# Three small edits to the order of work in a fused attention and mixer kernel: a transposed row by DMA, one relu on another engine, the last product's third tile whole

## The chip, the cores and the metric

The kernel runs on one core of one Trainium2 chip. A core has TensorE (PE in the profile; its weight loads are PEld), VectorE (DVE), ScalarE (ACT), GpSimd (POOL) and SyncE (SP, which here only issues transfers). PE writes to PSUM, in tiles of 128 partitions and up to 512 f32 to a bank; DVE and ACT read it. The metric is the device time of one execution in microseconds. The kernel before took 740.31 us, the median of three runs (740.12 to 741.42).

## The reference

Attention over 16 query and 4 key heads, then a mixer block over its output. B = 8 batches, S = 384 tokens, head size 64, model width 1024, hidden width 4096.

```python
# attention: x[b, s, h*64 + d]
k = np.repeat(k, 4, axis=1); v = np.repeat(v, 4, axis=1)
scores = np.matmul(q, k.transpose(0, 1, 3, 2)) / np.sqrt(64)
attn = np.exp(scores - np.max(scores, axis=-1, keepdims=True))
attn = attn / (np.sum(attn, axis=-1, keepdims=True) + 1e-09)
x = np.matmul(attn, v)                        # then heads side by side

# mixer
a1 = alpha1 * x + beta1
tok = np.einsum('ts,bsd->btd', w_tok, a1)     # across tokens
u = x + lam * tok
a2 = alpha2 * u + beta2
ch = np.maximum(a2 @ w_ch1, 0.0) @ w_ch2      # across channels
out = u + lam * ch
```

Inputs and output are f32; the kernel multiplies in bf16 and adds up in f32.

## The kernel before

**Tiles.** Tokens lie in NST = 3 tiles of 128, the model width in NP = 8 "rows" p of 128 columns (two heads each), the hidden width in 32 tiles of 128.

**Stages.** Batch 0's attention runs first. Batches 0 and 1 then go through `main(b)`: 32 hidden tiles, each of eight matmuls of 384 columns (L531) into a PSUM tile h with a relu on ACT (L540) or DVE (L542), and then the second layer (L569). The other six batches go in three pairs through `pair(i)`, which takes the two batches' channel layers as 2 x 2 block products with seven products in place of eight (a scheme of Strassen's kind). The first layer's products (L722) go into PSUM tiles X, Y and Z. The second layer's (L786) run in the order `PLACE2`, into tiles called C of 128 x 512, one for each token tile ms: 16 matmuls (t from 0 to 15) of 512 columns for each product and token tile.

**Work woven in.** While the channel layers of two batches run, the attention and the token mix of the next ones are made beside them. `side(b)` gives these pieces with unit numbers, and every `yield` of `main` and `pair` is one unit: at it, the pieces that are due are issued. The pieces of a row p are:

- `scores3`: matmuls (L279) into a tile from `three()` and an exp on ACT (L288). With `later` the third exp of a group is put off into a list.
- `av(p)`: matmuls (L315), then on DVE a reciprocal (L320), the division (L323) and the scaled input of the token mix (L328, L330). At its end the put-off exps are issued (L408, L409).
- `tok_flip(p)`: the token mix, nine matmuls of 128 columns (L340) into a tile from `three()`; DVE reads it (L347: u = x + tok) and scales it to a2 (L351). Then `spill(p)` writes u to the output by a transfer of SP (L243), and a2 is turned, so that channels lie on partitions: by a DMA transpose of SP (L362), or, where `by_pe(p)` says so, later by `turn(p)`.
- `turn(p)`: three transposes on PE (L427) into a tile from `three()`, and a copy on ACT (L429).

In the pairs the next odd batch (5 beside the first pair, 7 beside the second) has turns for its rows 5, 6 and 7, and so has batch 3, which is made beside batch 1's `main`. Nothing is woven into the third pair. Near the end of a pair's work the units are: 74 `turn(5)` and `tok_flip(6)`, 76 `tok_flip(7)`, 77 `turn(6)`, 79 `turn(7)`; the sums of the turned inputs for the next pair (`sums_a`, L586 to L588) follow from unit 76 on.

**PSUM in the second layer of a pair.** Two banks' worth of tiles belong to the pool `acc`; three more pools `sc0`, `sc1`, `sc2` have one tile of two banks each. `three()` hands these out in turn to scores, av, token mix and turns, and leaves sc0 out while `pairs["held"]` is set. Product 4 of the first two pairs is made in two halves (h = 0 with t from 0 to 7, h = 1 with t from 8 to 15), and its three token tiles stay open between them; the third (ms = 2) has sc0, taken at unit 76 in the middle of the tail above. A tile of a pool is given again only when the last reader of the tile before it has finished; the waits for this follow from the order in which tiles are asked for.

**Order.** The order of each engine's instructions is the order in which the code issues them; there is no scheduler that moves them.

**Which engine makes a relu.** A counter `exps[0]` is set by every exp: to 2 behind an exp of batches 1 to 7, to 0 in batch 0. Each hidden tile in `main` lowers it by one and goes to ACT when it is below zero, else to DVE (L538 to L543). So two relus behind an exp go to DVE.

**The last pair's end.** In the last pair every product is made in halves over h, and the products add up in the same PSUM tiles. Product 4 is the last of `PLACE2`. Its third token tile is held as two tiles, columns 0 to 383 (sc1) and 384 to 511 (sc2), so that the first can be finished while the second is multiplied. A finished tile is scaled on DVE (L794), added (L795) and written (L796).

Of the kernel before, what the change touches and what calls it, by code (L numbers as in the profile page):

```python
# [12 lines left out]
def kernel(  # L13
# [36 lines left out]
    NST = S // P  # L50
# [3 lines left out]
    NP = Hq // 2  # L54
    D1 = D + 1
    NPL = 2
# [58 lines left out]
    def by_tok(ap):  # L115
        return ap.rearrange("(p st) d -> p st d", st=NST)
# [91 lines left out]
    late, exps = [], [0]  # L208
# [20 lines left out]
    def side(b):  # L229
# [72 lines left out]
        def av_piece(p, hh):  # L302
            if hh == 0:
                if first:
                    avs[p] = bank([P, 2, NST, D1], "mm", "av")
                else:
                    avs[p] = one().rearrange("p k s -> p (k s)")[:, :2 * NST * D1].rearrange(
                        "p (h st d) -> p h st d", h=2, st=NST)
            av = avs[p]
            hk = (2 * p + hh) // G  # L310
            for sq in range(NST):
                m = NST * hh + sq
                for sk in range(NST):
                    k = (p * NST + sk) * NST + m // 2
                    nc.tensor.matmul(out=av[:, hh, sq, :], lhsT=ess[k // 4][:, m % 2, k % 4, :],  # L315
                                     rhs=vb[:, sk, hk, :], start=(sk == 0), stop=(sk == NST - 1))
            if hh == 0:
                return
            rinv = sb.tile([P, 2, NST, 1], f32, tag="rinv", name="rinv", bufs=1)
            nc.vector.reciprocal(out=rinv, in_=av[:, :, :, D:])  # L320
            if not first:
                xr[p] = sb.tile([P, NST, P], f32, tag="xr", name="xr", bufs=4)
            nc.vector.tensor_tensor(out=x_of(p).rearrange("p st (h d) -> p h st d", h=2), in0=av[:, :, :, :D],  # L323
                                    in1=rinv.to_broadcast([P, 2, NST, D]), op=MUL)
            if first:
                return
            t = sb.tile([P, NST, P], f32, tag="a1f", name="a1f", bufs=1)
            nc.vector.tensor_tensor(out=t, in0=x_of(p), in1=bc(g1, p), op=MUL)  # L328
            a1s[p] = sb.tile([P, NST, P], bf, tag="a1", name="a1", bufs=2)
            nc.vector.tensor_tensor(out=a1s[p], in0=t, in1=bc(h1, p), op=ADD)  # L330
# [74 lines left out]
        def av(p):  # L405
            av_piece(p, 0)
            av_piece(p, 1)
            while late:  # L408
                late.pop(0)()  # L409

        def tok_flip(p):
            tok(p)
            flip(p)
# [5 lines left out]
                a2_transpose(p)  # L419

        def by_pe(p):
            return b % 2 and p >= (NP - 3 if b > NPL else NP - 1)

        def turn(p):
            ps = three()[:, 0].rearrange("p a b -> p (a b)").bitcast(bf)[:, :S].rearrange("p (a b) -> p a b", a=NST)
# [166 lines left out]
    def spare(i):  # L592
        at = 24 * S + i % 3 * 1024
        return hTf[:, at:at + 1024]
# [43 lines left out]
    def free(slot):  # L638
        (w1_free if slot < RING else pad_free).append(slot)
        pump()  # L640
# [29 lines left out]
    def pair(i):  # L670
# [19 lines left out]
        def flush(n=9):  # L690
            while later and n:
                f, *a = later.pop(0)
                f(*a)
                n -= 1

        last = i == NB - 1
# [12 lines left out]
        for g in range(NH // 2):  # L709
            X, Y, snap = {}, {}, {}  # L710
            for k, (o, e) in enumerate(SEQ1):
                t = 2 * g + e
# [47 lines left out]
        def c_banks(ms):  # L760
            return [(0, 512, pairs["sc0"].tile([P, 2, 512], f32, tag="sc", name="C", bufs=1)[:, 0] if ms == NST - 1 else
                     acc.tile([P, 512], f32, tag="acc", name="C", bufs=2))]

        X = [c_banks(ms) if last else None for ms in range(NST)]
        snap = {}
        where = {2: (0, 0), 3: (0, 1), 7: (1, 1), 4: (1, 0)}
        for k, o in enumerate(PLACE2):
            whole = not last and o != 4
            for h in range(1 if whole else 2):
                for ms in range(NST):  # L770
                    if o == 4 and not last and 1 < 3 * h + ms < 5:
                        sum_w1(0, (5, 7, 6)[3 * h + ms - 2])
                    if last and (o, h) in ((6, 1), (7, 0)):
                        (lift_end if o == 7 else begin_end)(ms)
                    if last and (o, h, ms) == (7, 0, NST - 1):
                        X[ms] = [(c0, c1, pairs[sc].tile([P, 2, 512], f32, tag="sc", name="C", bufs=1)[:, 0, :c1 - c0])
                                 for sc, c0, c1 in (("sc1", 0, 384), ("sc2", 384, 512))]
                    if whole:
                        X[ms] = [(0, 512, acc.tile([P, 512], f32, tag="acc", name="C", bufs=2))]
                    elif not last and h == 0:  # L780
                        X[ms] = c_banks(ms)
                        pairs["held"] = ms == NST - 1
                    upto = NH if whole else 8 * h + 8
                    for (c0, c1, x), t in ((c, t) for c in X[ms] for t in range(8 * h, upto)):
                        slot, rhs = w2_slots[i, 4 * k + t // 4], w2_at[i, 4 * k + t // 4]
                        nc.tensor.matmul(out=x, lhsT=hid[:, t, LEFT2[o], ms * P:(ms + 1) * P],  # L786
                                         rhs=rhs[:, t % 4 * 512 + c0:t % 4 * 512 + c1],
                                         start=((not last or o in (1, 6, 7)) and t == 0), stop=(t == NH - 1),
                                         skip_group_check=True)
                        if t % 4 == 3 and ms == NST - 1 and c1 == 512 and not (o == 4 and slot >= RING):  # L790
                            free(slot)
                        if last and o == 4 and t == NH - 1:
                            e, v = ends[ms][:, c0:c1], spare(ms).bitcast(f32)[:, c0:c1]
                            tt(out=v, in0=x, in1=lam_t[:, c0:c1], op=MUL)  # L794
                            tt(out=e, in0=e, in1=v, op=ADD)  # L795
                            nc.sync.dma_start(out=by_tok(out[b0 + 1])[:, ms, c0:c1], in_=e)  # L796
                        if t % 4 == 3 and t < upto - 1 and c1 == 512:
                            q = 4 * ms + t // 4
                            if whole and o in (2, 6) and q in (2, 5, 8, 10):
                                sums_hid(o, (2, 5, 8, 10).index(q))  # L800
                            if t % 8 == 3 and later and (last or later[0][1] != 4):
                                flush(1)
                            yield 1
                    if k == ms == h == 0:
                        pad_free[:] = [RING + 1, RING + 2, RING]
                        pump()
                    if (whole or h == 1) and not (last and o == 4):
                        if o in (1, 6, 5):
                            q = ((1, 6, 5).index(o) * NST + ms) * 512
                            snap[o, ms] = snaps[:, q:q + 512]  # L810
                        else:
                            bb, dw = where[o]
                            t = snap[1, ms] if o == 7 else spare(ms).bitcast(f32)
                        for c0, c1, x in X[ms]:
                            if o == 1:
                                nc.scalar.copy(out=snap[o, ms], in_=x)
                            elif o in (6, 5):
                                tt(out=snap[o, ms], in0=x, in1=snap[1 if last or o == 6 else 6, ms], op=ADD)
                            elif o == 2 and last:
                                tt(out=t, in0=x, in1=lam_t[:, :512], op=MUL)  # L820
                            else:
                                base = {2: 1, 3: 1 if last else 5, 7: 5, 4: 6}[o]
                                tt(out=t[:, c0:c1], in0=x, in1=snap[base, ms][:, c0:c1], op=ADD)
                            if o == 7 and not last:
                                tt(out=snap[6, ms], in0=x, in1=snap[6, ms], op=ADD)
                        if o not in (1, 6, 5):
                            later.append((scaled, o, b0 + bb, ms, dw, t))
                    if last and o in (2, 6) and (h, ms) in ((0, 1), (0, 2), (1, 0), (1, 1)):
                        sums_hid(o, [(0, 1), (0, 2), (1, 0), (1, 1)].index((h, ms)))
                    yield 1  # L830
# [5 lines left out]
    with tc.manual_schedule(engines=order):  # L836
# [162 lines left out]
        for i in range(NB - 1):  # L999
            ps, c = NPL + i, NPL + 2 * i + 2  # L1000
# [56 lines left out]
```

## Time and profile before

| what | value |
| --- | --- |
| runs, median (lowest to highest) | 740.31 us (740.12 to 741.42) |
| the profiled execution | 740.56 us |
| its span, first to last instruction | 738.8 us |
| DMA bytes, mean rate | 151.32 MB, 205 GB/s |
| matmuls of the second layer in pairs (L786), busy | 168.0 and 69.9 us (by where the weights lie) |
| matmuls of the first layer in pairs (L722), busy | 70.2 + 70.2 us into X, 39.0 us into Z |
| exps (L288) on ACT | 126, 1023 ns each |

A profile is one execution taken by the hardware profiler. Its page has the busy time of each engine, the chain of work that ended last, and groups of instructions by line. The trace behind the page also answers for waits (which engine waited for which, how long) and gives a timeline. In the timeline a line begins with the start in microseconds from the span's start and the length; `x8` means eight instructions in a row, and `[0.66 <-DVE hT L542]` that the engine was idle for 0.66 us before it and what ended that. `128x384 bf16<-128x384 f32` are the sizes and types written and read. `SPq` is SP issuing transfers. A matmul's length contains its way through the array, so single ones are longer than the pace at which they follow each other: eight of 512 columns take 1.73 us when they follow back to back, 0.2165 each, and eight of 384 columns 1.30 us.

### The profile page before, as it was taken

How to read it: one execution, taken by the hardware profiler on the slowest of the kernel's cores; microseconds unless marked ns; L12 is line 12 of the kernel's file. 1: busy time of each engine (PE TensorE's matmuls, PEld its weight loads, DVE VectorE, ACT ScalarE, POOL GpSimd, SP SyncE). 2: the span in 40 equal slices, each digit the busy share in tenths (PEclk: the TensorE clock that was granted, in tenths of full speed). 3: DMA queues.
4: the chain of work that ended last, by engine and by line, in shares of the span. 5: the costliest groups of instructions: out<-in, count | busy, mean ns of one | idle time of the engine just before them, and what ended most of it. 6: DMA issues, size and time to landing. Idle time of an engine off the chain costs nothing.

```text
span 738.8 us, 14511 instructions
## 1 busy us (share of the span) xinstructions
PE 731.5 (99%) x5769; PEld 418.8 (57%) x5769; DVE 516.9 (70%) x995; ACT 324.1 (44%) x467; POOL 163.5 (22%) x211
## 2 busy tenths in 40 slices
PE   8999999999999999999999999999999999999997
PEld 5866555566555566655555566655555566654444
DVE  7763366467587889749777988847968988762354
ACT  7632431444333566653334366664343266660000
POOL 9434221420000232211013244020002222000011
PEclk9999999999999999999999999999999999999999
DMA  9999999999899999999989999998989999937965
GB/s 184 194 202 200 207 209 175 185 191 199 204 258 281 177 218 212 268 249 205 297 197 197 202 149 191 204 246 198 274 236 172 211 127 145 172 117 261 293 182 103
DMA packets 218017, 151.32 MB, mean 205 GB/s; under 512 B 88660, under 2 KB 197060, under 8 KB 217948
## 3 DMA queue, kind: packets, MB, share of 16 engines
q0 software_dynamic: 120304, 64.60, 66.6%
q1 hardware_dynamic: 97100, 85.39, 42.9%
q8 instruction: 45, 0.74, 0.4%
q10 hardware_dynamic: 544, 0.39, 0.2%
q14 instruction: 24, 0.20, 0.1%
HBM read 154.84 MB, written 38.27 MB: 261 GB/s over the span
## 4 chain that ended last, share of the span: by engine, by line
PE 95%; DVE 2%; DMA 1%; ACT 0%; issue 0%; DVEq 0%
PE C L786 30%; PE X L722 17%; PE h L531 10%; PE ch L569 10%; PE Y L722 8%; PE sc L279 5%; PE Z L722 4%; PE sc L315 4%; PE sc L340 3%; DMA ops<-a 1%; PE h L223 1%; PE tok L340 1%; PE av L315 0%; PE warm L841 0%; PE tp L265 0%; ACT hT L288 0%
## 5 line engine op out<-in xcount | busy, mean ns | idle before, releaser
L288 ACT ACTIVATE es<-sc 128x1024 bf16<-128x1024 f32 x126 | 121.4, 1023 | 155.9 <-PE sc L279 144.8
L786 PE MATMUL C<-w,arena 128*128 128x512 bf16 (+2 forms) x744 | 168.0, 372 | 0.0
L786 PEld LDWEIGHTS <-arena 128*128 128x128 bf16 x1040 | 94.8, 98 | 100.5 <-issue 5.1
L727 ACT ACTIVATE hT<-X,bias 128x384 f32<-128x384 f32 x144 | 83.7, 581 | 61.6 <-PE X L722 54.9
L722 PEld LDWEIGHTS <-w 128*128 128x128 bf16 x768 | 75.1, 98 | 50.0
L516 POOL DMA_DIRECT2D out_dram<-hT x33 | 28.7, 871 | 284.3 <-DVE hT L687 106.3
L569 PE MATMUL ch<-arena,hT 128*128 128x512 bf16 x384 | 90.8, 379 | 0.0
L185 POOL DMA_DIRECT2D w<-in_moe_w_ch_dram x68 | 62.8, 964 | 98.4 <-PE X L722 34.4
L531 PE MATMUL h<-ops,w 128*128 128x384 bf16 (+1 forms) x480 | 83.3, 327 | 0.8 <-DVE hT L542 0.7
L722 PEld LDWEIGHTS <-pad 128*128 128x128 bf16 x576 | 56.4, 98 | 37.2
L722 PE MATMUL X<-ops,w 128*128 128x384 bf16 x384 | 70.2, 326 | 0.0
L722 PE MATMUL X<-ops,pad 128*128 128x384 bf16 x384 | 70.2, 326 | 0.0
L786 PE MATMUL C<-pad,arena 128*128 128x512 bf16 (+2 forms) x296 | 69.9, 373 | 0.0
L531 PEld LDWEIGHTS <-w 128*128 128x128 bf16 x480 | 45.4, 98 | 30.4 <-issue 2.7
L569 PEld LDWEIGHTS <-hT 128*128 128x128 bf16 x384 | 34.8, 98 | 36.8 <-issue 2.5
L347 DVE TENSOR_TENSOR xr<-sc,xr 128x384 f32<-128x384 f32 x56 | 30.9, 552 | 23.4 <-PE sc L340 23.4
L315 PEld LDWEIGHTS <-es 128*128 128x128 bf16 x1008 | 38.2, 97 | 12.4
L340 PEld LDWEIGHTS <-wtokT 128*128 128x128 bf16 x576 | 37.5, 98 | 11.8 <-DVE a L330 0.8
L279 PE MATMUL sc<-qT,kT 64*128 64x384 bf16 (+2 forms) x576 | 42.0, 272 | 0.8 <-DVE xr L323 0.3
L320 DVE RECIPROCAL rinv<-sc 128x6 f32<-128x6 f32 x56 | 10.7, 192 | 44.3 <-PE sc L315 44.1
L315 PE MATMUL sc<-v,es 128*128 128x65 bf16 x1008 | 39.8, 193 | 0.0
L722 PE MATMUL Z<-ops,w 128*128 128x384 bf16 x192 | 39.0, 326 | 0.0
(138 smaller groups left out, 911.0 us busy)
## 6 DMA issues: line engine op xcount, KB each, us to landing
w<-in_moe_w_ch_dram POOLq DMA_DIRECT2D x68, 512.0 KB, 10.3
w<-w2s SPq DMA_DIRECT2D x60, 512.0 KB, 4.3
pad<-w2s SPq DMA_DIRECT2D x24, 512.0 KB, 8.1
out_dram<-xr SPq DMA_DIRECT2D x56, 192.0 KB, 6.1
out_dram<-hT POOLq DMA_DIRECT2D x33, 256.0 KB, 5.7
arena<-in_moe_w_ch_dram POOLq DMA_DIRECT2D x16, 512.0 KB, 20.0
w2s<-arena SPq DMA_DIRECT2D x28, 256.0 KB, 5.0
q_raw<-in_q_dram POOLq DMA_DIRECT2D x28, 192.0 KB, 10.4
```

What stands on the lines that cost most here:

```text
L185: nc.gpsimd.dma_start(out=w1[:, w1_slots[c]], in_=w1src[:, :, c * CW * P:(c + 1) * CW * P])
L279: nc.tensor.matmul(out=sc[:, hh, k % 4:k % 4 + n], lhsT=kT[r, 2 * p // G, BLK[hh][sk], :], rhs=qT[r, p, st:st + n, :], start=True, stop=True)
L288: nc.scalar.activation(out=e, in_=sc, func=EXP, scale=scale_qk)
L315: nc.tensor.matmul(out=av[:, hh, sq, :], lhsT=ess[k // 4][:, m % 2, k % 4, :], rhs=vb[:, sk, hk, :], start=(sk == 0), stop=(sk == NST - 1))
L340: nc.tensor.matmul(out=ps[:, tt, :], lhsT=wtokT[:, st, tt * P:(tt + 1) * P], rhs=a1s[p][:, st, :], start=(st == 0), stop=(st == NST - 1 an ...
L347: nc.vector.tensor_tensor(out=u, in0=ps, in1=u, op=ADD)
L516: nc.gpsimd.dma_start(out=at, in_=o, accum_op=ADD)
L531: nc.tensor.matmul(out=ps[:, :n], lhsT=w1[:, w1_slots[c], dt, j * P:(j + 1) * P], rhs=a2T[:, dt, :n], start=(dt == 0), stop=(dt == NDT - 1))
L569: nc.tensor.matmul(out=ps, lhsT=hT[:, nt, ms * P:(ms + 1) * P], rhs=w2[:, row(nt)[0], row(nt)[1], cs], start=(i == 0), stop=(i == NNT - 1))
L722: nc.tensor.matmul(out=ps, lhsT=tb[g, o][:, dt, e * P:(e + 1) * P], rhs=opb(LEFT1[o])[:, dt], start=(o in (1, 2, 7) and dt == 0), stop=(dt ...
L727: nc.scalar.activation(out=snap[o, e], in_=ps, func=IDENT, bias=hi if o == 5 else lo)
L786: nc.tensor.matmul(out=x, lhsT=hid[:, t, LEFT2[o], ms * P:(ms + 1) * P], rhs=rhs[:, t % 4 * 512 + c0:t % 4 * 512 + c1], start=((not last o ...
```

## The change

Three edits.

1. Behind a put-off exp the counter is set to 1 and not left at 2, so one relu and not two goes to DVE after it.
2. `by_pe` takes rows 6 and 7, and no longer row 5, in batches 3, 5 and 7. Row 5's a2 is turned by a DMA transpose of SP (L362), issued right behind its spill. `turn(5)`, with its tile from `three()`, is no longer issued.
3. In the last pair's product 4 the third token tile is left out in the first half (h = 0) and gets all its 16 t in the second: columns 0 to 383 for t from 0 to 15, then columns 384 to 511.

```diff
@@ av
             while late:
                 late.pop(0)()
+                exps[0] = 1
@@ by_pe
-            return b % 2 and p >= (NP - 3 if b > NPL else NP - 1)
+            return b % 2 and p >= (NP - 2 if b > NPL else NP - 1)
@@ pair, second layer
             whole = not last and o != 4
+            tail = last and o == 4
             for h in range(1 if whole else 2):
-                for ms in range(NST):
+                for ms in range(NST - (tail and not h)):
...
                     upto = NH if whole else 8 * h + 8
-                    for (c0, c1, x), t in ((c, t) for c in X[ms] for t in range(8 * h, upto)):
+                    for (c0, c1, x), t in ((c, t) for c in X[ms]
+                                           for t in range(0 if tail and ms == NST - 1 else 8 * h, upto)):
```

## The prediction

> **What bounds the kernel now.** I read the page's busy list and chain first, then TensorE's (PE's) waits, then the timeline around each place that the diff touches.
>
> ```profile
> span 738.8 us, 14511 instructions
> PE 731.5 (99%) x5769; PEld 418.8 (57%) x5769; DVE 516.9 (70%) x995; ACT 324.1 (44%) x467; POOL 163.5 (22%) x211
> PE 95%; DVE 2%; DMA 1%; ACT 0%; issue 0%; DVEq 0%
> ```
>
> PE is busy in 99% of the span and carries 95% of the chain. So only three things change the time: PE work that goes or comes, a new PE wait, and what lies behind the last matmul. PE's waits, largest first (total us, times, longest):
>
> ```profile
> PE warm L841 <- DVE wtokT L844: 1.5, 1, 1.5
> PE h L531 <- DVE hT L542: 0.7, 1, 0.7
> PE sc L279 <- DVE xr L323: 0.3, 1, 0.3
> PE sc L279 <- ACT hT L288: 0.3, 1, 0.3
> ```
>
> They sum to 2.8 us, so a new wait is not swallowed by a later one: it goes to the end nearly whole. Line numbers are those of the kernel before.
>
> **Edit A: row 5 of batches 3, 5 and 7 turned by a transfer.** Per batch it removes three PE transposes (L427), one ACT copy (L429) and one call of `three()`, and adds a DMA_TRANSPOSE (L362) on SP's queue right behind row 5's spill (L243). The last pair has no side work, so there are three places: batch 3 (about 235 us) and the turns at 406.97 (batch 5) and 580.14 (batch 7). The timeline of the first pair's place (start, length, engine, line, operation):
>
> ```profile
> 406.97 0.33 PE L427 MATMUL sc<-ident,obuf 128*128 128x128 bf16 x3
> 407.13 0.67 PE L340 MATMUL sc<-a,wtokT 128*128 128x128 bf16 x9
> 407.33 0.48 ACT L429 COPY ops<-sc 128x384 bf16<-128x384 bf16 x1 [2.47 <-PE sc L427]
> 407.64 1.89 PE L786 MATMUL C<-pad,arena 128*128 128x512 bf16 x8
> ...
> 409.24 0.55 DVE L347 TENSOR_TENSOR xr<-sc,xr 128x384 f32<-128x384 f32 x1
> 409.37 0.66 PE L340 MATMUL sc<-a,wtokT 128*128 128x128 bf16 x9
> ```
>
> The work removed is small: the next instruction starts 0.16 us after the turn (407.13 − 406.97), since a matmul's 0.33 includes its pipeline. Three turns are worth −0.48.
>
> What the turn leaves behind is larger. `three()` hands out sc0, sc1, sc2 in rotation. At this place the order was: turn of row 5, token mix of row 6, the tile C of the third token tile of product 4 (always on sc0). Before, the turn took sc0, so C waited only for the ACT copy, done at 407.81; C's first matmul is the fifth of the eight issued from 407.64 (four matmuls of ms=1 come first; eight take 1.73), at 407.64 + 4 × 0.2165 = 408.51. With the turn gone, the token mix of row 6 moves onto sc0, and C can start only when DVE has read it: that is L347 at 409.24, which ends at 409.79. The changed kernel's instructions say the same: C's first matmul waits for that L347. L347 doesn't come earlier, because DVE runs without a gap from 403.20 to there (1.93 of 2.00 us busy in 406 to 408, 1.90 in 408 to 410; two rounds of L320, L323, L328, L330 with an L687 between them lie ahead of it); the removed ACT copy isn't in its queue. PE is ready at 408.51 − 0.16 = 408.35 and starts at 409.79 + 0.06 (a semaphore's way, as between other DVE ends and PE starts) = 409.85. That is 1.50 of waiting, 1.34 later than before. In the second pair:
>
> ```profile
> 580.81 1.89 PE L786 MATMUL C<-pad,arena 128*128 128x512 bf16 x8
> 582.42 0.55 DVE L347 TENSOR_TENSOR xr<-sc,xr 128x384 f32<-128x384 f32 x1
> ```
>
> before 580.81 + 0.87 = 581.68, after 582.42 + 0.55 + 0.06 = 583.03: 1.35 later. Both with the −0.16 inside: **+2.69**. Behind the waiting matmul all of PE is queued: the rest of product 4, the token mix of row 7 (409.37 becomes about 410.72), the turns of rows 6 and 7. DVE's L347 of row 7 goes from 410.90 to about 411.44, so DVE loses 0.54 where PE loses 1.34, and the sums for the next pair (L586 to L588) get more slack against PE, not less. Batch 3 has no C tile in that rotation and gives its **−0.16** alone.
>
> The transfers' price. SP is idle at all three places (about 233.5, 404.0 and 577.2), and the queue is almost empty there. An issue takes 1.2 to 3.0 us of SP; the landings of such transfers run from 2.4 by 5.1 (median) to 9.5 us:
>
> ```profile
> L362 SPq DMA_TRANSPOSE ops<-obuf x26: 1227/1298/2283, 327.9 to 570.8; - x26
> DMA to landing us min/median/max: 2.4/5.1/9.5
> 238.35 0.56 DVE L351 TENSOR_TENSOR a<-xr,vecs 128x384 bf16<-128x384 f32 x1
> ```
>
> In the pairs the first reader is the sum L586 at 411.96, 8 us after the issue: nothing below a landing of 8, up to 1.5 on DVE at 9.5, which its 1.3 us of slack hides. In batch 3 `a2` has two buffers, so row 7's L351 (238.35) must wait for row 5's transfer: 4.9 us after its issue for DVE; PE is reached only from about 6.7. I take 0, nearest the median, and keep 0 to +2.8 (9.5 − 6.7).
>
> By the Trainium skill ("TensorE: Matmul & The Clock Gate", section "Back-to-back issue gap") a sustained N=128 matmul issues about every 81 ns; this trace has 53 (three in 0.16). By the page's figure the nine turns would be worth an estimated −0.73 instead of −0.48. The row decides.
>
> **Edit B: `exps[0] = 1` behind a put-off exp.** In batch 1's first half (two places, about 150 and 177 us) the second of two relus goes from DVE to ACT. The second place:
>
> ```profile
> 180.65 0.61 DVE L542 TENSOR_SCALAR hT<-h,bias 128x384 bf16<-128x384 f32 x1
> 181.32 1.46 PE L531 MATMUL h<-ops,w 128*128 128x384 bf16 x8 [0.66 <-DVE hT L542]
> 181.78 0.61 DVE L542 TENSOR_SCALAR hT<-h,bias 128x384 bf16<-128x384 f32 x1
> ```
>
> PE waits 0.66 for a bank that the first relu reads until 181.26. The second relu's data are ready at about 180.15 and ACT is idle from 178.53 (the end of an exp) to 182.82, so on ACT it ends at 180.15 + 0.58 = 180.73; in the changed kernel the next h takes that bank and PE starts at 180.79: **−0.53** (bounds 0 and −0.66). At the first place PE's 0.3 is for the first relu, which stays on DVE: 0.
>
> **Edit C: the last product's third token tile whole, at the end.** The number and size of the matmuls stay; ms 0 and 1 finish 1.73 us (eight 512-column matmuls) earlier. The tail before:
>
> ```profile
> 733.01 3.65 SPq L796 DMA_DIRECT2D out_dram<-ends  x4
> 734.62 0.55 DVE L794 TENSOR_TENSOR hT<-C,vecs 128x384 f32<-128x384 f32 x1
> 735.21 0.56 DVE L795 TENSOR_TENSOR ends<-ends,hT 128x384 f32<-128x384 f32 x1
> 735.68 0.28 DVE L794 TENSOR_TENSOR hT<-C,vecs 128x128 f32<-128x128 f32 x1
> ```
>
> PE ends at 734.99 (729.63 + 5.36), but the last 128 columns wait for DVE until 735.68. Now sixteen instead of eight 128-column matmuls lie between the end of the 384 columns and PE's end, so they are done at 734.99 − 16 × 0.0535 = 734.13 and L794 starts at 734.17 instead of 734.62; all behind it shifts by the same: **−0.45**. Bounds: −0.3 (if the last transfer isn't shortened by it) and −0.9, if the last transfer also finds the queue emptier, as ms 1's leaves earlier.
>
> **Sum:** 2.69 − 0.16 − 0.53 − 0.45 = **+1.55**. The profiled execution took 740.56 (738.8 span + 1.76 around it), 0.25 above the median of the runs, 740.31. So profiled about 742.1, median 740.31 + 1.55 = **741.9**. About 0.2%, 1.5 us, is what a measurement of this kernel can tell from no change; the forecast lies on that border.
>
> **Rivals.**
> 1. *The bank wait doesn't bite: faster.* If L347 of row 6 ran earlier, or C found a free bank, the change is −0.48 − 0.53 − 0.45 = −1.46: 738.9. For it: the row 6 mix itself ends on PE at 407.8, so only DVE's queue holds L347 back. Against: DVE has no gap there, in either pair. If half of the wait appears the time is 740.2. Chance 0.10 for below 739.6, 0.15 for a part of the wait (739.6 to 741).
> 2. *Batch 3's transfer lands late (slower still).* The decisive point is a landing of 6.7 us; at 9.5 row 7's L351 and with it PE lose 2.8: 744.7. For it: the maximum of 9.5 is on record and software queues take two thirds of the DMA time. Against: 21 and 10 GB/s in the two slices around the issue. Chance 0.10.
> 3. *The relu gain is missing*, as the next h gets the old bank: 742.4. Chance 0.12.
> 4. *A pause lowers PE's clock.* The granted clock is 1.00 until 737.5 and then 0.52, 2.5 us after the last matmul (734.99); the 0.66 pause at 181 left it at 1.00. If a pause of 1.5 us lowered it as well, for the 2.5 us that it took to fall there, half speed would cost 1.25 more in each pair: 744.4. Chance 0.05.
> The Trainium skill (the page above, section "A second HAM failure mode: psum-queue depth-cycling") has repeated short idle gaps between banks as a way to lose the clock; no pause of 1.5 us inside this trace tests it.
>
> **How the numbers follow.** The forecast itself has 0.48 (741 to 742.9 by the bounds of edits B and C and ±0.4 on the waits). The time is the forecast's, 741.9. Low: with rival 1 whole outside, 739.9; high: half of rival 2, 743.6. Faster than 738.8: rival 1's whole only, 0.07. Of forecast and rival 3, a little over half lies above 741.8, all of rivals 2 and 4 do: slower 0.50. The rest, with the part wait, is no change: 0.43.
>
> **What would show it.** Right: PE waits of about 1.5 us at L786 near 409 and 582 put down to DVE L347, none at 181.3 above 0.2, the last L794 of 384 columns about 0.8 us before PE's end, nine turns fewer. Wrong: no such wait, a wait at batch 3's token mix near 239, or a granted clock below 1.00 before 730.

## The result and the profile after

The changed kernel takes 742.67 us (median of seven runs, 742.06 to 744.18) against 740.31 us (seven runs, 740.07 to 741.42): +2.36 us, a ratio of 1.0032 with a 95% interval of 1.002 to 1.0044. It is slower by 0.3%, inside the range of the forecast (739.9 to 743.6) and 0.8 us above the 741.9 that was forecast. The profiled execution took 743.58 us. Line numbers of the changed kernel are one higher than before from L411 on and three higher from L786 on (L542 is L543, L786 is L789, L794 is L797).

The page of the changed kernel, its span, busy times and chain by engine:

```profile
span 741.8 us, 14438 instructions
PE 726.7 (98%) x5701; PEld 418.1 (56%) x5760; DVE 515.3 (69%) x993; ACT 323.6 (44%) x466; POOL 163.9 (22%) x211
PE 78%; DVE 7%; DMA 7%; issue 4%; POOL 2%; SPq 1%; ACT 0%; POOLq 0%; DVEq 0%
```

PE had 95% of the chain; now it has 78%, and DVE and DMA have 7% each. (In this trace 68 matmul records fewer are counted than before, though only nine were taken away; weight loads, 5760 and 5769, count them better.) PE's waits of the changed kernel, total, times and longest in us:

```profile
PE C L789 <- DVE xr L347: 2.7, 2, 1.4
PE warm L844 <- DVE wtokT L847: 1.5, 1, 1.5
PE Y L723 <- DVE arena L730: 0.6, 1, 0.6
PE h L532 <- DMA ops<-a: 0.4, 1, 0.4
...
PE Y L723 <- DVE arena L736: 0.3, 1, 0.3
...
PE h L532 <- DVE hT L543: 0.2, 1, 0.2
```

The first line is the forecast's wait, in both pairs. The two waits at Y and the one for `ops<-a` (a transposed row of a2, at 133 us) are new and were not forecast. The timeline of the changed kernel at the first pair's place:

```profile
406.23 0.67 PE L340 MATMUL sc<-a,wtokT 128*128 128x128 bf16 x9
406.73 1.03 PE L789 MATMUL C<-pad,arena 128*128 128x512 bf16 x4
408.50 0.55 DVE L347 TENSOR_TENSOR xr<-sc,xr 128x384 f32<-128x384 f32 x1
409.11 1.02 PE L789 MATMUL C<-pad,arena 128*128 128x512 bf16 x4 [1.35 <-DVE xr L347]
```

Eight matmuls of C stood here without a break before. Now the four of the second token tile run, and the four of the third begin 0.06 us after L347's end (409.05). Row 6's token mix had left PE at 406.9; DVE read it 1.6 us later. The 1.35 in the bracket counts from the end of the matmul before. By their pace of 0.2165 us the four would have begun at 407.60 (406.73 + 0.87), so PE lost 1.51 us here, of which the missing turn gives back 0.16. The second pair is the same:

```profile
582.51 1.03 PE L789 MATMUL C<-pad,arena 128*128 128x512 bf16 x4
584.28 0.55 DVE L347 TENSOR_TENSOR xr<-sc,xr 128x384 f32<-128x384 f32 x1
584.89 1.02 PE L789 MATMUL C<-pad,arena 128*128 128x512 bf16 x4 [1.35 <-DVE xr L347]
```

The relu's place, where PE had waited 0.66 us at 181.32:

```profile
180.12 0.58 ACT L541 ACTIVATE hT<-h,bias 128x384 bf16<-128x384 f32 x1 [1.61 <-PE h L532]
180.61 0.61 DVE L543 TENSOR_SCALAR hT<-h,bias 128x384 bf16<-128x384 f32 x1
180.75 1.46 PE L532 MATMUL h<-ops,w 128*128 128x384 bf16 x8
```

ACT's relu ends at 180.70 and PE goes on at 180.75, before DVE's relu is done. The tail:

```profile
737.34 0.56 DVE L797 TENSOR_TENSOR hT<-C,vecs 128x384 f32<-128x384 f32 x1 [1.18 <-PE C L789]
737.58 0.61 PE L789 MATMUL C<-w,arena 128*128 128x128 bf16 x8
738.40 0.28 DVE L797 TENSOR_TENSOR hT<-C,vecs 128x128 f32<-128x128 f32 x1
738.72 0.29 DVE L798 TENSOR_TENSOR ends<-ends,hT 128x128 f32<-128x128 f32 x1
```

PE ends at 738.19, and the 384 columns' first step begins 0.85 us before that. The last 128 columns' first step starts 0.21 us after PE's end, against 0.69 before.

**Where the time went.** Matching PE's instructions of two traces one by one gives the lead or lag at each moment. The table has how much was lost (+) or gained (−) in each stretch against the profiled execution before, in us. "Closing" is the time from PE's last matmul to the end of the span, 3.78 us before; the columns add up to the difference of the spans within 0.03 (stretches without a change of 0.03 or more are left out). The other rows are of the experiments below.

| kernel | to 175 | relu, 181 | batch 3's turn | first pair, 409 | weights, 440 to 490 | second pair, 560 to 620 | closing | span |
| --- | --- | --- | --- | --- | --- | --- | --- | --- |
| changed | −0.04 | −0.53 | −0.17 | +1.34 | +1.27 | +1.33 | −0.18 | +3.02 |
| a_only | −0.58 | 0 | −0.17 | +1.33 | +0.51 (and +0.23 to 560) | +1.32 | +0.35 | +3.00 |
| b_only | −0.57 | −0.53 | 0 | 0 | 0 | 0 | +0.01 | −1.07 |
| c_only | −0.23 | 0 | 0 | 0 | 0 | 0 | −0.45 | −0.68 |
| all_skip | −0.34 | −0.53 | −0.17 | +0.02 | 0 | +1.40 | −0.17 | +0.21 |
| pause_only | −0.71 | 0 | 0 | +1.33 | +0.10 | +1.32 | 0 | +2.06 |
| bc | +0.25 | −0.53 | 0 | 0 | +0.37 | 0 | −0.47 | −0.38 |
| bc_b3 | +1.18 | −0.53 | −0.17 | 0 | 0 | 0 | +0.34 | +0.81 |
| skip_order | +0.21 | −0.54 (and +0.38 at 188) | −0.17 | +0.02 | +0.43 | 0 | −0.17 | +0.19 |
| bc_2 | +0.58 | −0.53 | 0 | 0 | +0.09 | 0 | −0.46 | −0.31 |
| bc_b3_2 | −0.26 | −0.53 | −0.17 | 0 | 0 | 0 | +0.33 | −0.61 |
| pairs_skip | +1.90 | −0.54 | 0 | +0.02 | 0 | +1.27 | −0.10 | +2.56 |
| bc_b3_end | −0.09 | −0.53 | −0.17 | 0 | 0 | 0 | −0.45 | −1.23 |

The stretch to 175 us holds one relu of the second edit (at 154 us) and nothing else of the change, and it differs by −0.71 to +1.90 from one execution to the next: single spans can't be compared to better than that. Two things make the largest of these differences. At 133 us PE waits for the landing of a transposed row (`ops<-a`): 2.19 us in pairs_skip, 1.23 in bc_2, 0.44 in the changed kernel, and not in the others. In bc_b3 PE waits 1.20 us at 10.8 for DVE, and the granted clock is 0.50 from 11.9 to 15.3 us; no other trace shows it below 1.00 before PE's last matmul. The columns for the relu, the turn and the two bank waits can be compared: each edit gives the same within 0.02 every time. The weights' column can't. Medians below are over 5 to 12 executions.

The +1.27 at 440 to 490 in the changed kernel is this (changed kernel, timeline, DVE and PE):

```profile
459.92 0.69 DVE L627 TENSOR_TENSOR pad<-w 128x1024 bf16<-128x1024 bf16 x1 [2.99 <-DMA w<-in_moe_w_ch_dram]
461.86 1.46 PE L723 MATMUL Y<-ops,pad 128*128 128x384 bf16 x8 [0.65 <-DVE arena L730]
```

and before:

```profile
457.76 0.69 DVE L626 TENSOR_TENSOR pad<-w 128x1024 bf16<-128x1024 bf16 x1 [1.62 <-DMA w<-in_moe_w_ch_dram]
```

DVE's weight sums of the second pair wait for a chunk of weights on GpSimd's queue, which lands 14.2 us after its issue before and 15.8 after; behind them stands L730, which PE needs. Before, PE was just not reached.

### The profile page after: what moved, and what is told of

Its sections match the earlier page's. It is cut to its first block, busy times and chain, and to the rows that moved or that the text cites. A ratio compares the mean times of both kernels' runs of the same rounds, so it can differ in the third digit from the quotient of the medians.

```text
span 741.8 us, 14438 instructions
## 1 busy us (share of the span) xinstructions
PE 726.7 (98%) x5701; PEld 418.1 (56%) x5760; DVE 515.3 (69%) x993; ACT 323.6 (44%) x466; POOL 163.9 (22%) x211
## 4 chain that ended last, share of the span: by engine, by line
PE 78%; DVE 7%; DMA 7%; issue 4%; POOL 2%; SPq 1%; ACT 0%; POOLq 0%; DVEq 0%
PE C L789 26%; PE X L723 13%; PE h L532 10%; PE ch L570 8%; PE Y L723 7%; PE sc L279 4%; DMA w<-in_moe_w_ch_dram 4%; PE sc L315 3%; PE Z L723 3%; PE sc L340 3%; DMA ops<-a 2%; DVE xr L323 1%; DVE a1f L328 1%; DVE xr L347 1%; POOL w L185 1%
## 5 line engine op out<-in xcount | busy, mean ns | idle before, releaser
L789 PE MATMUL C<-w,arena 128*128 128x512 bf16 (+2 forms) x711 | 163.7, 372 | 1.6 <-issue 0.3
L789 PEld LDWEIGHTS <-arena 128*128 128x128 bf16 x1040 | 94.8, 98 | 103.5 <-issue 8.3
L570 PE MATMUL ch<-arena,hT 128*128 128x512 bf16 x366 | 87.6, 379 | 0.9 <-issue 0.3
L789 PE MATMUL C<-pad,arena 128*128 128x512 bf16 (+2 forms) x288 | 69.8, 373 | 3.1 <-DVE xr L347 2.7
L347 DVE TENSOR_TENSOR xr<-sc,xr 128x384 f32<-128x384 f32 x56 | 30.9, 552 | 25.0 <-PE sc L340 24.9
L723 PE MATMUL Y<-ops,w 128*128 128x384 bf16 x192 | 39.0, 326 | 0.3 <-DVE arena L736 0.3
```

The lines of the kernel that those rows point to most:

```text
L347: nc.vector.tensor_tensor(out=u, in0=ps, in1=u, op=ADD)
L570: nc.tensor.matmul(out=ps, lhsT=hT[:, nt, ms * P:(ms + 1) * P], rhs=w2[:, row(nt)[0], row(nt)[1], cs], start=(i == 0), stop=(i == NNT - 1))
L723: nc.tensor.matmul(out=ps, lhsT=tb[g, o][:, dt, e * P:(e + 1) * P], rhs=opb(LEFT1[o])[:, dt], start=(o in (1, 2, 7) and dt == 0), stop=(dt ...
```

## The experiments

All are compared with the kernel before, run beside them on the same chip; its medians there were 740.26 to 740.43 us. Differences are of medians.

**a_only: the transferred row alone.**

```diff
-            return b % 2 and p >= (NP - 3 if b > NPL else NP - 1)
+            return b % 2 and p >= (NP - 2 if b > NPL else NP - 1)
```

> The kernel before with the transferred row 5 alone. Theory 1 (bank wait): two PE waits of about 1.35 us at the matmul of C for DVE L347, near 409 and 582, so +2.53 us (2.69 - 0.16) on the kernel before. Theory 2 (the lateness of a weight chunk in the second pair near 460, 1.3 us in the profile of the changed kernel, comes from the row's transfers or from the pause): +3.3 to +3.8 and a PE wait at Y near 460. If the transfers are what costs and not the banks: about +1 and no wait for L347.

743.83 us, +3.43, ratio 1.0048 (1.0036 to 1.006). The waits for L347 are there and cost 1.33 and 1.32. The rest, 0.9 above the forecast, is not explained by them, but 0.35 of it is the closing, without any edit of the tail. The time is in theory 2's range (+3.3 to +3.8), and PE does wait at Y near 464, but only 0.30 us; pause_only, below, takes the pause and the transfers apart.

**b_only: the relu alone.**

```diff
                 late.pop(0)()
+                exps[0] = 1
```

> The kernel before with the relu edit alone. Theory 1: -0.53 us, and PE's wait of 0.66 us near 181 for DVE L542 gone or below 0.2. Rival (the next h keeps the old bank): no change, the wait stays. If a wait at Y near 460 appears here as well, the late weight chunk has nothing to do with the transferred row.

739.83 us, −0.57, ratio 0.9995 (0.9986 to 1.0005). The timing alone doesn't separate this from no change; the trace does: −0.53 at the relu and nothing else behind it.

**c_only: the tail alone** (the third part of the change's diff).

> The kernel before with the third token tile of the last product whole and last, alone. Theory 1: -0.45 us (-0.3 to -0.9); DVE's multiplication of 384 columns starts 0.8 us before the last matmul ends, and nothing else in the trace moves. Rival (the last transfer's landing sets the end, whenever the earlier pieces leave): within 0.1 of no change.

739.78 us, −0.62, ratio 0.9995 (0.9986 to 1.0004). In the trace the closing is 3.33 us instead of 3.78, −0.45, and no other stretch behind the opening moves.

**all_skip: the changed kernel with the rotation kept.**

```diff
+        def skip_bank():
+            if pairs:
+                pairs["turn"] = (pairs["turn"] + 1 + (pairs["turn"] == 2 and pairs["held"])) % 3
...
                     if by_pe(p):
                         put((36, 39, 41)[p - NP + 3], turn, p)
+                    elif b % 2 and p == NP - 3:
+                        put(36, skip_bank)
```

> The changed kernel, but where turn(5) of batches 5 and 7 was, the rotation of the three PSUM pools is moved on by one without a tile, so that the token mix of row 6 does not take sc0. Nothing else differs. Theory 1: no PE wait for L347 at C, so 2 x 1.34 less than the changed kernel and -0.48 - 0.53 - 0.45 = -1.5 against the kernel before. Theory 2 with the transfers as the cause of the late chunk: -0.7 and a wait at Y near 460; with the pause as its cause: -1.5 and no such wait. If the bank was not what PE waited for, it stays near +2.

740.86 us, +0.46, ratio 1.0008 (0.9999 to 1.0017). The waits for L347 are gone, so the bank was what PE waited for. But the gain is far from whole: the first pair gives +0.02 in place of +1.34, and the second pair loses 1.40 in another place. The 0.16 of the turn doesn't stay either: row 7's token mix now begins 0.06 us after DVE has made its input (L330, until 408.28; the mix at 408.34), and DVE is no earlier for the missing turn. Timeline of this run, SP, DVE and PE:

```profile
576.01 2.28 SPq L362 DMA_TRANSPOSE ops<-obuf  x1
...
585.95 0.56 DVE L593 TENSOR_TENSOR ops<-ops 128x768 bf16<-128x768 bf16 x1 [1.74 <-DMA ops<-obuf]
...
591.61 0.32 PE L729 MATMUL Y<-ops,w 128*128 128x384 bf16 x1 [1.22 <-DMA out_dram<-xr]
```

L593 (L586 before) is the first sum, which reads rows 0, 1, 4 and 5 of the odd batch: it waits for row 5's transfer, the three sums and those behind them on DVE are late, and PE stands at the second product of the next pair. (The last bracket names a spill, but PE's 591.61 comes 0.05 us after row 3's L594, which that product reads, has ended at 591.56.) The packets of SP's queue, which the trace has one by one, tell why the transfer is late. Row 5's transfers, us:

```
run         issued    first packet  last packet   issue to last
changed     232.92    234.20        235.32        2.4
changed     403.11    407.62        410.20        7.1
changed     578.89    584.93        586.64        7.8
all_skip    402.81    407.23        409.86        7.1
all_skip    576.01    582.34        585.35        9.3
```

Between the issue and the first packet the queue moves the weights fetched before it (4096-byte packets at 576 to 581) and the spill (512-byte packets). SP's instruction stream was idle at the issue; its queue was not.

**pause_only: the wait without the transfer** (the kernel before, with `skip_bank` as above).

```diff
                     if by_pe(p):
                         put((36, 39, 41)[p - NP + 3], turn, p)
+                    if b % 2 and p == NP - 3:
+                        put(36, skip_bank)
+                        put(36, skip_bank)
```

> The kernel before, its turn(5) kept; behind it the rotation of the three PSUM pools is moved on by two, so that the token mix of row 6 takes sc0, as in the changed kernel. No transfer is added and no relu or tail moved. Theory 1 (the bank costs 1.34 in each pair, and what the row alone cost beyond the forecast, 0.9 of its 3.43, comes from its transfers): +2.7, two waits for L347. Theory 2 (the pause itself makes later weight chunks late against PE, near 460): +3.5, with a wait at Y near 460 to 475.

743.02 us, +2.76, ratio 1.0035 (1.0023 to 1.0048): theory 1, within 0.1. PE's waits of this run are two for each pair:

```profile
PE sc L340 <- ACT ops L433: 1.1, 2, 0.6
PE C L793 <- DVE xr L347: 0.9, 2, 0.5
```

Row 6's token mix first waits for the turn's copy on sc0, and then C for L347. L347 begins when DVE comes to it (at 408.53, which is the 409.24 of the kernel before less this execution's lead of 0.71), and it sets when C goes on; so the loss is the same 1.33 and 1.32. The weights column has +0.10. Against a_only, which has the same two losses, 0.7 us less are lost, which speaks for the transfers and against the pause as the source of the rest.

**bc: the relu and the tail, no transfer** (both edits as above).

> The relu edit and the tail edit together, row 5 turned by PE as in the kernel before. They touch places far apart, so the sum of what each gave alone: -0.57 - 0.62 = -1.2. If the earlier PE only runs into a later wait (weight chunks), -0.6 or less.

739.24 us, −1.02, ratio 0.999 (0.9981 to 0.9998). This is below the kernel before, and 0.2 short of the −1.2 expected; in its trace the relu (−0.53) and the closing (−0.47) are whole, and 0.37 is lost at the weights.

**bc_b3: that, and batch 3's transfer alone.**

```diff
-            return b % 2 and p >= (NP - 3 if b > NPL else NP - 1)
+            return b % 2 and p >= (NP - 2 if b == NPL + 1 else NP - 3 if b > NPL else NP - 1)
```

> As before this one, and row 5 of batch 3 alone turned by a transfer. Theory 1 (batch 3's transfer is in time): -0.16 more, -1.35 in all. Rival (a2's two buffers make row 7 wait for the transfer): +0.3 or more against the run without it, with a PE wait near 239.

739.85 us, −0.41, ratio 0.9995 (0.9986 to 1.0004): 0.6 above bc, as the rival had it, but not by its reason. No PE wait stands near 239; batch 3's turn gives −0.17. What differs is the closing: 4.12 us, where bc has 3.32.

**skip_order: the rotation kept, and row 5's sum last.**

```diff
-            for j, u in ((0, 76), (2, 79), (3, 81)):
-                put(ps, 1, u, sums_a, j, 1 if j else 2)
+            for j, u in ((0, 76), (2, 79), (3, 81), (1, 81)):
+                put(ps, 1, u, sums_a, j)
...
-                for dt in range(NDT // 2):
+                dts = (0, 2, 3, 1) if i and not g else (0, 1, 2, 3)
+                for dt in dts:
```

> The run with the rotation kept (all three edits), but the sums of rows 1 and 5 are made last, behind those of rows 3 and 7, and the first products of the next pair take their four parts in the order 0, 2, 3, 1. In the trace of the rotation-kept run the packets of row 5's transfer ran from 582.3 to 585.4, 9.3 us after its issue, and the first sum (which needs row 5) waited 1.74 us for it. Theory T (the transfer's landing at that sum is what kept the rotation-kept run from -1.5): no DVE wait for that transfer, no PE wait at Y near 591, -1.3 to -1.7. Rival (something else, such as the weight chunks, costs it): it stays near +0.5.

739.8 us, −0.46, ratio 0.999 (0.9981 to 0.9999). The waits for the transfer and at Y near 591 are gone: the second pair gives +0.02 instead of +1.40, and the median falls by 0.9 against all_skip (each against the kernel before of its own series). So the landing at that sum was the cost in the second pair. It doesn't reach the −1.3 expected: 0.28 is the closing. In this execution another 0.43 is lost at the weights and 0.38 at 188 us, where PE waits for the landing of a transposed q (`[0.32 <-DMA qT<-q_raw]`); the relu's gain itself is whole.

**bc_2 and bc_b3_2: both again, side by side.**

> The relu and tail edits again, row 5 by PE throughout: -1.0 to -1.2 as before, as the base for the next two on the same chip.

> Again with row 5 of batch 3 alone by a transfer. In its first trace nothing near 235 waits for that transfer (packets from 235.4 to 236.4, landed before row 7's L351), and the loss sat in the opening, before any edit. If the 0.6 above the run without it was such an accident: within 0.25 of that run (-0.16 expected). If batch 3's transfer costs it in most executions: again +0.4 to +0.8 above it.

739.58 and 739.89 us, −0.78 and −0.47 (ratios 0.9992, 0.9983 to 1.0001, and 0.9996, 0.9987 to 1.0005): 0.3 apart this time. The first is short of the −1.0 to −1.2 expected, and the second lies between its two theories. Over both series, 22 executions each, the medians are 739.35 and 739.88, 0.5 apart. The profile's difference is the same in both: closing 3.32 against 4.12, +0.80, and −0.17 at the turn, together +0.63.

**pairs_skip: the rotation kept, transfers in the two pairs alone** (with `skip_bank` as in all_skip).

```diff
-            return b % 2 and p >= (NP - 2 if b > NPL else NP - 1)
+            return b % 2 and p >= (NP - 2 if b > NPL + 1 else NP - 3 if b > NPL else NP - 1)
```

> All three edits with the rotation kept, but row 5 of batch 3 by PE: the transfers are those of the two pairs alone. If batch 3's transfer costs 0.6: about -0.1 (0.46 - 0.6). If the whole shortfall of the rotation-kept run is the late landing in the pairs: +0.5 to +0.6.

741.53 us, +1.17, ratio 1.0019 (1.0007 to 1.0032), above both expectations. The late landing is there (+1.27 in the second pair), so it belongs to the pairs' transfers. The profiled execution also lost 1.90 before 175 us (its wait of 2.19 at 133), where bc and bc_2 have the same instructions and lost 0.25 and 0.58. The terms in the table from the relu on add up to +0.65; what lifts the median by 0.5 more is not explained.

**bc_b3_end: the closing.** The closing goes with the number of transfers that SP issues. Without the tail edit it is 3.78 us with as many as before and 4.13 with three more (a_only). With the tail edit it is 3.33 with as many, 4.12 with one more, 3.68 with two and 3.61 with three. At the end of the program SP waits for the semaphores of all transfers, in a fixed order. Transfers issued by SP take eight of them in turn. The trace's records of these waits, us after PE's last matmul, by semaphore:

```
semaphore                  107   109   111   112   113   115   116   118
bc_b3 (last one on 107)    2.42  2.49  2.56  2.94  3.02  3.09  3.15  3.21
c_only (last one on 118)   1.34  1.41  1.50  1.57  1.64  2.03  2.21  2.42
```

In both the last transfer is issued 0.85 us after PE's end and its last packet moves until 2.06. With the last one on the first semaphore, seven waits still follow the landing; with it on the last, they are gone through before. The run moves one early transfer to GpSimd, so that the count is as before:

```diff
-            nc.sync.dma_start(out=t, in_=by_tok(out[b0 + 1])[:, ms, :512])
+            (nc.sync if ms else nc.gpsimd).dma_start(out=t, in_=by_tok(out[b0 + 1])[:, ms, :512])
```

> Relu edit, tail edit and batch 3's row 5 by a transfer, as twice before; one of SP's transfers (the first load of ends in the last pair, L679) is issued by GpSimd, so that the number of transfers issued by SP and ACT, and with it the semaphore of the last one, is as in the kernel before. Theory E (the closing waits of SP go through eight semaphores in a fixed order; the last transfer's stood last before, first with one transfer more, and then seven waits still follow its landing): the time from PE's last matmul to the end of the span falls from 4.12 to 3.32 us, and the median to -1.0 to -1.3 against the kernel before. Rival (the 0.5 comes from batch 3's transfer itself or from chance): the closing stays above 3.9 and the median within -0.3 to -0.6.

739.52 us against 740.43, −0.91, ratio 0.9985 (0.9977 to 0.9994). The closing is 3.33. The last DVE instruction and SP's drain (the closing line: how often, shortest, median and longest ns, first and last start) in bc_b3:

```profile
736.00 0.29 DVE L798 TENSOR_TENSOR ends<-ends,hT 128x128 f32<-128x128 f32 x1
...
L1055 SPq DRAIN  x3: 7/7/13, 738.8 to 739.1; - x3
```

and in bc_b3_end:

```profile
734.75 0.29 DVE L798 TENSOR_TENSOR ends<-ends,hT 128x128 f32<-128x128 f32 x1
...
L1055 SPq DRAIN  x3: 7/7/13, 736.7 to 737.0; - x3
```

From the last DVE start to SP's first drain it is 2.8 and 1.95 us. Theory E holds in the trace. In the medians bc_b3_end is 0.4 to 0.5 better than the two runs of bc_b3, each against the kernel before of its own series. This is less than the 0.8 of the trace and short of the −1.0 to −1.3 expected, and about equal to bc.

## Why the prediction came out as it did

- **The bank wait.** Right in mechanism, place and size: +1.34 and +1.35 forecast, +1.34 and +1.33 in the trace, +2.76 in time when it was made alone. L347 did not come earlier, and the wait went to the end whole. In the changed kernel PE's clock was granted at 1.00 until after its last matmul, so rival 4 falls for these two pauses. That a short pause never lowers it is not shown: in bc_b3's opening a low clock did follow 1 us after the wait of 1.20 us. The 2.5 us that the rival took from one trace is 2.0 to 5.4 in the other traces, from the last matmul to the clock's fall. The Trainium skill's page "TensorE: Matmul & The Clock Gate" (section "A second HAM failure mode: psum-queue depth-cycling") tells of a clock that swings when PE idles often between bank changes; the waits for banks in the pairs show no such swing in any run here.
- **The turns.** −0.16 each forecast; −0.17 in batch 3. Inside the pairs it does not stay: with the rotation kept the first pair ends at +0.02, since row 7's token mix waits for DVE instead. In the changed kernel it is inside the +1.34. By the Trainium skill (the same page, section "Back-to-back issue gap", 81 ns at N=128) an estimate for three is −0.24. The trace has −0.17, or 57 ns each.
- **The relu.** −0.53 forecast and −0.53 in the trace; rival 3 falls.
- **The tail.** −0.45 forecast and −0.45 in the trace alone. In the changed kernel only −0.18 of it arrives.
- **What failed: the transfers at nothing.** "SP is idle at all three places, and the queue is almost empty there" was true of batch 3 (2.4 us from issue to last packet, so rival 2 falls) and false in the pairs (7.1 and 7.8, where the text's middle value was 5.1). I read the idle instruction stream and a few slices of traffic as an empty queue; the weights fetched just before were still in it. The kernel before shows it: there their 4096-byte packets move on SP's queue from 402.0 to 407.7 and from 575.0 to 579.8 us, around the places of the two issues. In the changed kernel this cost nothing at the sums: the first starts at 587.52, 0.9 after the last packet. With the rotation kept the packets end later after the issue (9.3 us in all_skip and 9.1 in pairs_skip, against 7.8), and DVE is ready for the first sum earlier after it (8.2 against 8.6); there it costs 1.3 to 1.4. Why the packets come later there is not shown, only that the weights ahead of them end 5.0 and 4.7 us after the issue, against 3.7. So the gain that rival 1 promised, −1.46, was not there either: +0.46 was measured. Keeping the rotation removes the bank wait in both pairs and brings the late landing in the second.
- **What was missing: the closing.** The added transfers were priced by issue and landing, not by its place among SP's closing waits: three more transfers cost 0.28 at the end (3.61 against 3.33).
- **The sum.** In the profiled execution −0.53 − 0.17 + 1.34 + 1.33 − 0.45 = +1.52 is the forecast's sum of +1.55. The closing's 0.27 and the late weights' 1.27 make up the rest of the 3.02. In time it is +2.36, of which 1.8 are accounted for by the forecast's terms and the closing. That the time still lies inside the forecast's own 741 to 742.9 is in part luck: this margin was for the relu, the tail and the size of the waits, and these came out as forecast; of the 0.8 above 741.9 the closing's 0.27 is a term that the sum did not have, and the rest stays open.

**Open:** the remaining half microsecond. Adding each version's terms from the table without the opening and the weights (a_only: −0.17 + 1.33 + 1.32 + 0.35 = 2.83, measured 3.43) leaves 0.5 to 0.6 over in three of the five versions with transfers in the pairs (the changed kernel, a_only, pairs_skip), 0.4 in skip_order if its 0.38 at 188 is left out too (else nothing), nothing in all_skip, and −0.2 to +0.25 in those without. The changed kernel and a_only are 1.07 apart, and the relu and the closing give 1.06 of it, so what is left over is the same in both. In each version alone it lies inside the 95% interval of the time (+1.5 to +3.3 for the changed kernel). The weights' lateness near 460 would fit, with +1.27, +0.51 and +0.43 in three of the four, and so would the wait at 133 in pairs_skip and the changed kernel. But one execution of each was profiled; pairs_skip had nothing at the weights, and bc, without any such transfer, had +0.37. It was not shown that the change causes either.

The fastest versions are bc, without the transferred row (−1.02 and −0.78), and bc_b3_end (−0.91). The transferred row never paid in the pairs: the 0.16 us that it takes from PE are given back at once.

## What to carry to other kernels

When an edit removes a user of a rotating buffer, follow which buffer every later user gets: the work taken away here was worth 0.16 us and the shift cost 1.34, because a tile that must be ready at once came to stand behind the busiest reader. Before pricing the removal of such a wait, look for the next thing that is late at the same place; here the next one cost 1.4 in one of the two pairs. Here a transfer's time counted from when its queue reached it (first packet 4.4 to 6.3 us after the issue in the pairs), not from when the issuing engine was free.

## What was not expected of the hardware

The program's last transfer cost up to 0.80 us more or less by which of eight semaphores it had, since SP's closing waits go through them in a fixed order, some 0.06 to 0.4 us each. One transfer more at 235 us shifted this by 0.80 us, almost five times what that edit took from PE (0.17); a trace shows it as the time between the last matmul and the end of the span. The start, up to 175 us, differed by up to 2.6 us between executions of kernels that differ there by one relu at most, and by 1.4 between two executions of the same kernel (bc_b3, +1.18 and −0.26).
